# Unused matmuls in every gap of TensorE's plan, and a plan that reckons with half clock behind gaps

## The chip, the core and the metric

One core of one Trainium2 chip runs the whole program. The metric is the device time of one execution in microseconds. 0.2% of it, about 2.2 us, is what a measurement of this kernel can tell from no change.

## What is computed

An attention layer with a complex decaying state, cut to its recurrence, and behind it two feed-forward layers (FFN) over 3072 tokens, all in float32 (B = 4, H = 8, S = 768, D = 48):

```python
for t in range(S):
    ar, ai = a_re_n[:, :, t, :, None], a_im_n[:, :, t, :, None]   # normalised to at most 0.999
    new_re = ar * S_re - ai * S_im
    new_im = ar * S_im + ai * S_re
    S_re, S_im = new_re + k[:, :, t, :, None] * v[:, :, t, None, :], new_im
    y[:, :, t] = einsum('bhd,bhde->bhe', q[:, :, t], S_re)
x = y.transpose(0, 2, 1, 3).reshape(3072, 384)
h = x @ w_in;  x = (h * sigmoid(h)) @ w_out                        # 384 -> 2048 -> 384
h = x @ w_in2
g = where(h >= 1, h, where(h <= -1, 0, (h + 1) ** 2 / 4));  out = g @ w_out2
```

## The kernel before

The attention is cut into 12 units of 256 tokens (three in a row for each batch, all 8 heads at once). A unit normalises the decays, scans them into running products P (VectorE, mostly many small products in a chain), and forms Q times P and K divided by P. TensorE transposes these (`ptr`, from Q and from A), multiplies scores (`psc`), VectorE masks them (`AT`), TensorE multiplies the values (`py`) and the state of the unit (`pS`). Two small transposes serve the scan: `pt` (waits for RR) and `pe` (waits for X and brings back E).

The first FFN runs in 6 jobs of two units, 512 tokens each. Each float32 operand is split into a high and a low part of type fp32r, and every product takes three matmuls. A job has 16 steps f: 9 matmuls into `ph` (hidden layer), a gate on ScalarE that gives gH, a subtraction on VectorE that gives gL, and 9 matmuls that add into three sums `acc0` to `acc2`, which stay open from f = 0 to f = 15. The weights come as float64 bit patterns and are turned into float32 by VectorE, ScalarE and, for five of them, TensorE (`pw`). The second FFN (`pacc`) is alike and starts when the first has ended.

The order of instructions is set at build time by the class `Plan`. Each piece of work is a generator that asks for an engine, a duration and an earliest time. `go` always takes the request whose planned start plus its lag is smallest, and the instruction is written into its engine's queue at that moment. On the chip each queue runs in that order. So the planner's durations decide the order, and only that: on the chip an instruction starts when its engine and its data are there.

Unused matmuls exist already: the generator `awake` writes matmuls of 128x512 on the tile `junk` until the first FFN starts, each planned 3 us ahead of what it would wait for. The planner doubles TensorE's durations only until 16 of these have been planned (`cold`). The rows of the profile call these instructions `junk`.

Of the kernel before, what the change touches and what calls it, by code (L numbers as in the profile page):

```python
# [7 lines left out]
F32 = mybir.dt.float32  # L8
F32R = mybir.dt.float32r
I32 = mybir.dt.int32  # L10
# [10 lines left out]
PE, DVE, ACT, SP = "PE", "DVE", "ACT", "SP"  # L21


class Plan:
# [6 lines left out]
    def __init__(self):  # L31
        self.free = dict.fromkeys((PE, DVE, ACT, SP, "DMA"), 0.0)
        self.at = {}
        self.runs = []
        self.table = "exp"
        self.cold = lambda: False
        self.log = []
        self.rings = {"t": [2], "pa": [PAB], "ph": [PHB], "gH": [3], "gL": [3], "xq": [1], "sc": [4]}

# [30 lines left out]
    def dma(self, t, kb):  # L70
        b = self.free["DMA"] = max(self.free["DMA"], t + 1.4) + kb / 260.0
        return b + 0.8

    def go(self):
        while self.runs:
            best, moved = None, False
            for r in list(self.runs):
                while r in self.runs and (got := self.ready(r[2])) is not None:
                    self.step(r, got)
                    moved = True  # L80
                if r not in self.runs or isinstance(r[2], str) or len(r[2]) == 2:
                    continue
                e, us, t, *more = r[2]
                b = max(self.free[e], t)
                key = b + (more[1] if len(more) > 1 else r[0]())
                if best is None or key < best[0]:
                    best = key, b, r
            if best is None:
                if moved or not self.runs:
                    continue  # L90
                raise RuntimeError(str([(r[1].__name__, r[2]) for r in self.runs]))
            _, b, r = best
            e, us, t, *more = r[2]
            if e == PE and self.cold():
                us *= 2
            if more and more[0] and more[0] != self.table:
                self.table = more[0]
                us += 1.3
            self.log.append((b, e, us, r[1].__name__))
            self.free[e] = b + us  # L100
            self.step(r, b + us + 0.12)


def MM(n):
    return 0.69 if n == 512 else 0.37
# [704 lines left out]
class Ffn:  # L810
    def __init__(self, nc, tc, pools, w, plan):
        self.nc, self.tc, self.w, self.plan = nc, tc, w, plan
        self.W = [[None, None] for _ in range(8)]
        self.f = -1
        self.at = 0
        self.cp, self.wp, self.pp, self.dp, self.hp = pools
        self.cst = self.cp.tile([128, 3], F32, name="cst")
        for i, x in enumerate((-1.0, 0.5, 1.0)):
            nc.gpsimd.memset(self.cst[:, i:i + 1], x)
        self.fl_big = self.cp.tile([128, 32], F32, name="fl_big")  # L820

    def fetch(self, k, t0=0.0):
# [100 lines left out]
    def one(self, n, u, x, dst, tx, behind):  # L923
        nc, wp, pp, plan = self.nc, self.wp, self.pp, self.plan
        G, acc = {}, []
        p, N = u[0] // 2, 256 * len(u)
        part = N / 512
        o = u[0] % 2 * 256
        x = x[:, :, :, o:o + N]
        xH, xL = x[:, 0], x[:, 1]  # L930

        def outs(f):
            t0 = yield f"g{n}.{f}"
            if n == 0:
                t0 = max(t0, (yield f"w{f // 2 * 2 + 1}"))
            if f == 0:
                if n:
                    t0 = max(t0, (yield f"xo{n - 1}"))
                acc.extend(pp.tile([128, 512], F32, name=f"acc{j}", tag=f"acc{j}")[:, 0:N] for j in range(3))
            gH, gL, hH, hL = G.pop(f)  # L940
            oH, oL = self.wslices(f, 1)
            for j in range(3):
                w = slice(j * 128, (j + 1) * 128)
                t1 = yield PE, MM(N), t0
                nc.tensor.matmul(acc[j], oH[:, w], gH, start=f == 0, stop=False)  # L945
                nc.tensor.matmul(acc[j], oH[:, w], gL, start=False, stop=False)  # L946
                nc.tensor.matmul(acc[j], oL[:, w], gH, start=False, stop=f == 15)  # L947
                if f == 15:
                    T.append(t1)
            plan.drop("gH", hH, t1)  # L950
            plan.drop("gL", hL, t1)
            if u[-1] == UNITS - 1 and f % 2:
                plan.mark(f"used{f // 2 * 2 + 1}", t1)
            if f == 15:
                plan.add(XO, copies())

        T = []

        def copies():
            x2 = self.hp.tile([128, 3, 512], F32, name="x2", tag=f"x{p % 2}")[:, :, o:o + N]  # L960
            for j in range(3):
                t1 = yield ACT, 0.14 + 0.42 * part, T[j] + 0.2
                nc.scalar.copy(x2[:, j], acc[j])
                t2 = yield SP, 0.5, t1
                nc.sync.dma_start(dst[j * 128:(j + 1) * 128], x2[:, j])
            plan.mark(f"xo{n}", t1)
            t2 = plan.dma(t2, 262 * part)
            if u[-1] % 2:
                plan.mark(f"ffn{p}", t2)
                plan.mark(f"free x{p}", t2)  # L970

        def gate(f, ph, h, t1):
            hH, tH = yield "gH", 1
            gH = self.hp.tile([128, 512], F32R, name="gH", bufs=3)[:, 0:N]
            hL, tL = yield "gL", 1
            gL = self.hp.tile([128, 512], F32R, name="gL", bufs=3)[:, 0:N]
            t1 = yield ACT, 0.2 + 0.42 * part, t1 + 0.2, "silu"
            nc.scalar.activation(ph, ph, AF.Silu)  # L978
            t1 = yield ACT, 0.14 + 0.42 * part, max(t1, tH)
            nc.scalar.copy(gH, ph)  # L980
            t1 = yield DVE, 0.08 + 0.53 * part, max(t1, tL)
            nc.vector.tensor_tensor(gL, ph, gH, ALU.subtract)  # L982
            plan.drop("ph", h, t1)
            G[f] = gH, gL, hH, hL
            plan.mark(f"g{n}.{f}", t1)

        for f in range(16):
            tw = 0.0
            if n == 0:
                self.f = f  # L990
                tw = yield f"w{f // 2 * 2}"
            self.at = 1 + (u[0] + f / 16 * len(u)) / 2
            h, tf = yield "ph", 1
            ph = pp.tile([128, 512], F32, name="ph", tag="ph", bufs=PHB)[:, 0:N]
            t1 = yield from self.hidden(ph, f, xH, xL, max(tx, tw, tf), N)
            if u[-1] == UNITS - 1 and f % 2:
                plan.mark(f"used{f // 2 * 2}", t1)
            if f == 15 and u[-1] % 2:
                plan.mark(f"y{p}", t1)
            plan.add(GLAG, gate(f, ph, h, t1))  # L1000
            behind.append(outs(f))
            if len(behind) > DEEP:
                yield from behind.pop(0)
# [135 lines left out]
UR = 5  # L1139
SEP = 12  # L1140
SL = 0.75
AW = 0.25
WL = 1.4
WE = 0.45
FL = 0.2
# [12 lines left out]
def all_units(tc, plan, at, ff, xd2, out, fp, bad):  # L1158

    nc, wp = tc.nc, at.wp  # L1160
# [29 lines left out]
    def loada(i):  # L1190
        t = yield f"kT{i - 2}"
        t = max(t, (yield f"free{i - 2}"))
        yield from at.loada(i, t)
# [35 lines left out]
        yield "two1"  # L1229
        yield from flag_bad(nc, fp, at.pp, at, ff, plan, bad)  # L1230

    def awake():

        t = yield "P0"
        junk = at.pp.tile([128, 512], F32, name="junk", tag="acc0")
        while ff.f < 0:
            t = yield PE, AW, t - 3.0
            nc.tensor.matmul(junk, at.nid, at.nid.unsqueeze(1).to_broadcast([128, 4, 128]), start=True, stop=True)
            plan.at["warm"] = plan.at.get("warm", 0) + 1

    def second(k):
        t = max((yield f"used{k}"), (yield f"h{UNITS - 1}"))
# [6 lines left out]
        for k in range(n, 16, 2):  # L1249
            yield from second(k)  # L1250

    plan.cold = lambda: ff.f < 0 and plan.at.get("warm", 0) < 16
    with tc.manual_schedule(engines=None):
        plan.add(0.0, loads())
        for i in range(1, UNITS):
            if i > 1:
                plan.add(0.0, loada(i))
            plan.add(0.0, loadq(i, 0))
            plan.add(0.0, loadq(i, 1))
            plan.add(0.0, loadv(i))  # L1260
        for i in range(UNITS):
            plan.add(at.lag(i), at.unit(i, x))
            plan.add(0.0, at.knat(i))
        for n in range(3):
            me = [0]
            plan.add(urgent(me), weights(me))
        plan.add(behind, ffn())
        for n in range(2):
            plan.add(SL, seconds(n))
        for m in range(PAIRS):  # L1270
            plan.add(0.5, ff.prep(m, xd2[:, m * 512:(m + 1) * 512], ys))
        plan.add(FL, second_ffn())
        plan.add(0.5, flag())
        plan.add(1.2, awake())
        plan.go()


# [73 lines left out]
```

## Time and profile before

| | before |
|---|---|
| median of 3 runs | 1095.72 us (1095.23 to 1096.23) |
| the profiled execution's own time | 1097.16 us |
| its span, first to last instruction | 1095.5 us |
| mean granted TensorE clock | 0.978 |
| TensorE busy | 1018.3 us (93%) |
| VectorE busy | 797.7 us (73%) |
| ScalarE busy | 682.7 us (62%) |

Times in the views count from the span's start. Neighbouring matmuls overlap in the rows, so the time of one is read from a run of them. A row's bracket gives the engine's idle time before it, and what ended it.

### The profile page before, as it was taken

What the parts mean: (1) busy time and instruction counts of PE and PEld (TensorE: products, weight loads), DVE (VectorE), ACT (ScalarE), POOL (GpSimd) and SP (SyncE); (2) the same over time, 40 slices, a digit from 0 to 9 for tenths busy, and PEclk for the clock granted to TensorE, in tenths of its full rate; (3) what the DMA queues carried; (4) which work ended last, traced back from release to release, by engine and by line L of the source; (5) the groups of instructions that cost most, each with busy time, mean ns of one, the idle gap of its engine ahead of it and who ended that gap; (6) DMA issues with size and microseconds to landing.
All of it is one profiled execution on the core that took longest, in us unless ns stands there. A gap on an engine that the chain in (4) does not pass through costs nothing.

```text
span 1095.5 us, 14607 instructions
## 1 busy us (share of the span) xinstructions
PE 1018.3 (93%) x5486; PEld 840.2 (77%) x5486; DVE 797.7 (73%) x1492; ACT 682.7 (62%) x1048; POOL 1.4 (0%) x16
## 2 busy tenths in 40 slices
PE   0598698989999999999999999999999999999997
PEld 0476486778888888888888888887887878888896
DVE  6989999978888788898984179876556565555553
ACT  4456787768778686777846366665455454454443
POOL 0000000000000000000000000000000000000000
PEclk9789999899999999999999999999999999999999
DMA  5412350133131331313122165402002020000100
GB/s 215 156 40 87 137 202 22 43 124 116 37 102 65 124 98 69 116 37 102 65 80 74 40 218 182 173 1 59 1 1 58 1 58 1 14 15 1 29 1 32
DMA packets 55150, 82.03 MB, mean 75 GB/s; under 512 B 34592, under 2 KB 40480, under 8 KB 55072
## 3 DMA queue, kind: packets, MB, share of 16 engines
q1 hardware_dynamic: 54640, 80.53, 22.3%
q8 instruction: 45, 0.74, 0.3%
q10 hardware_dynamic: 432, 0.49, 0.1%
q14 instruction: 33, 0.27, 0.1%
HBM read 61.34 MB, written 17.30 MB: 72 GB/s over the span
## 4 chain that ended last, share of the span: by engine, by line
PE 72%; DVE 9%; ACT 8%; issue 1%; DMA 0%; SPq 0%; ACTq 0%; DVEq 0%
PE pacc L1086 16%; PE ph L903 10%; PE ph L905 10%; PE ph L904 10%; PE acc L945 5%; PE acc L946 5%; PE acc L947 5%; PE py L466 4%; PE psc L444 3%; PE ptr L372 2%; PE pS L537 2%; ACT L224 1%; ACT r L224 1%; DVE tt L176 1%; ACT ph L978 1%
## 5 line engine op out<-in xcount | busy, mean ns | idle before, releaser
L903 PE MATMUL ph<-x,wi 128*128 128x512 f32 x576 | 230.4, 400 | 3.2 <-DMA x<-xq 3.2
L904 PE MATMUL ph<-x,wi 128*128 128x512 f32 x576 | 225.7, 392 | 0.0
L905 PE MATMUL ph<-x,wi 128*128 128x512 f32 x576 | 225.6, 392 | 0.0
L1086 PE MATMUL pacc<-gH,wo 128*128 128x512 f32 x480 | 159.4, 390 | 0.0
L903 PEld LDWEIGHTS ph<-x,wi 128*128 128x128 f32 x576 | 109.0, 189 | 27.4 <-issue 2.4
L905 PEld LDWEIGHTS ph<-x,wi 128*128 128x128 f32 x576 | 108.7, 189 | 23.2
L904 PEld LDWEIGHTS ph<-x,wi 128*128 128x128 f32 x576 | 109.0, 189 | 20.7
L946 PE MATMUL acc<-gL,wo 128*128 128x512 f32 x288 | 113.9, 396 | 7.8 <-DVE gL L982 7.8
L945 PE MATMUL acc<-gH,wo 128*128 128x512 f32 x288 | 117.9, 409 | 0.0
L947 PE MATMUL acc<-gH,wo 128*128 128x512 f32 x288 | 114.0, 396 | 0.0
L1107 ACT ACTIVATE c<-c,cst 128x512 f32<-128x512 f32 x96 | 69.5, 724 | 63.8 <-DVE c L1104 63.8
L1109 DVE TENSOR_TENSOR g<-c,l 128x512 f32<-128x512 f32 x96 | 66.5, 693 | 56.4 <-ACT c L1107 56.3
L1113 DVE TENSOR_TENSOR gL<-g,gH 128x512 fp32r<-128x512 f32 x96 | 66.5, 692 | 55.0 <-ACT gH L1111 53.9
L1104 DVE TENSOR_SCALAR c<-ph 128x512 f32<-128x512 f32 x96 | 66.3, 690 | 52.8 <-ACT l L1102 52.6
L1086 PEld LDWEIGHTS pacc<-gH,wo 128*128 128x128 f32 x480 | 90.1, 188 | 18.6
L1102 ACT ACTIVATE l<-ph,cst 128x512 f32<-128x512 f32 x96 | 65.8, 685 | 60.1 <-PE ph L905 59.9
L978 ACT ACTIVATE ph<-ph 128x512 f32<-128x512 f32 x96 | 57.5, 599 | 72.2 <-PE ph L905 71.7
L1111 ACT CAST gH<-g 128x512 fp32r<-128x512 f32 x96 | 59.6, 621 | 64.3 <-DVE g L1109 64.3
L982 DVE TENSOR_TENSOR gL<-ph,gH 128x512 fp32r<-128x512 f32 x96 | 65.5, 686 | 45.6 <-ACT gH L980 45.2
L1086 PE MATMUL pacc<-gL,wo 128*128 128x512 f32 x240 | 94.6, 394 | 1.7 <-DVE gL L1113 0.8
L946 PEld LDWEIGHTS acc<-gL,wo 128*128 128x128 f32 x288 | 55.0, 191 | 18.2 <-DVE gL L982 8.3
L947 PEld LDWEIGHTS acc<-gH,wo 128*128 128x128 f32 x288 | 54.9, 191 | 11.9
(176 smaller groups left out, 1715.7 us busy)
## 6 DMA issues: line engine op xcount, KB each, us to landing
raw<-in_w_dram SPq DMA_DIRECT2D x32, 768.0 KB, 5.9
A<-in_a_dram SPq DMA_DIRECT2D x12, 768.0 KB, 4.7
kd<-A SPq DMA_DIRECT2D x10, 768.0 KB, 4.0
KN<-kd SPq DMA_DIRECT2D x20, 384.0 KB, 3.8
qt<-in_qk_dram SPq DMA_DIRECT2D x12, 384.0 KB, 3.1
kt<-in_qk_dram SPq DMA_DIRECT2D x12, 384.0 KB, 4.6
vt<-in_vn_dram SPq DMA_DIRECT2D x24, 192.0 KB, 2.5
xd<-x SPq DMA_DIRECT2D x18, 256.0 KB, 2.2
```

Source lines behind the costliest of these rows:

```text
L903: nc.tensor.matmul(ph, iH[:, j], xH[:, j], start=j == 0, stop=False, skip_group_check=True)
L904: nc.tensor.matmul(ph, iH[:, j], xL[:, j], start=False, stop=False, skip_group_check=True)
L905: nc.tensor.matmul(ph, iL[:, j], xH[:, j], start=False, stop=j == 2, skip_group_check=True)
L945: nc.tensor.matmul(acc[j], oH[:, w], gH, start=f == 0, stop=False)
L946: nc.tensor.matmul(acc[j], oH[:, w], gL, start=False, stop=False)
L947: nc.tensor.matmul(acc[j], oL[:, w], gH, start=False, stop=f == 15)
L978: nc.scalar.activation(ph, ph, AF.Silu)
L1086: nc.tensor.matmul(o, l, r, start=f == 0 and k == 0, stop=f == 15 and k == 2)
L1104: nc.vector.tensor_scalar(c, ph, 1.0, -1.0, ALU.min, ALU.max)
L1107: nc.scalar.activation(c, c, AF.Square, bias=self.cst[:, 1:2], scale=0.5)
L1109: nc.vector.tensor_tensor(g, c, l, ALU.add)
L1113: nc.vector.tensor_tensor(gL, g, gH, ALU.subtract)
```

## The change

Four things are changed.

- `awake` and `cold` go. In their place `Plan.idle` looks, at every TensorE request, at the planned gap ahead of it (8 us of it at most). From 0.6 us on it writes unused matmuls for the gap, one per 0.235 us, half as many for the first 4 us if the planned clock is low.
- `Plan.clocked` keeps a list of planned busy time and doubles a TensorE duration while the planned clock counts as low. This holds for the whole plan, not only for the start.
- An unused matmul multiplies by a tile of zeros. Until the first sum of a job has begun, `fill` writes nothing (or, before the first FFN, to the tile `junk`); from then to f = 15 it adds its zeros into the open sum acc0.
- Ahead of these, one memset of the zero tile.

```diff
-        self.cold = lambda: False
+        self.slow, self.past, self.fill = True, [], None
...
+    def idle(self, b):
+        g = min(b - self.free[PE], 8.0) - 0.1
+        if g < AK or b < 25.0:
+            return
+        n = int(g / AW if not self.slow else min(g, 4.0) / AW / 2 + max(0.0, g - 4.0) / AW)
+        if n and self.fill(n):
+            self.past.append((b - g, b))
+
+    def clocked(self, b, us):
+        p = self.past
+        while p and p[0][1] < b - 4.0:
+            p.pop(0)
+        n = sum(y - max(x, b - 4.0) for x, y in p)
+        self.slow = n < (3.7 if self.slow else 2.2)
+        us *= 1 + self.slow
+        p.append((b, b + us))
+        return us
...
-            if e == PE and self.cold():
-                us *= 2
-            if more and more[0] and more[0] != self.table:
+            if e == PE:
+                self.idle(b)
+                us = self.clocked(b, us)
+            elif more and more[0] and more[0] != self.table:
...
+            if f % 15 == 0:
+                self.open = None
...
+            if f == 0:
+                self.open = [acc[0], n]
...
-AW = 0.25
+AW = 0.235
+AK = 0.6
...
-    def awake():
-        t = yield "P0"
-        junk = at.pp.tile([128, 512], F32, name="junk", tag="acc0")
-        while ff.f < 0:
-            t = yield PE, AW, t - 3.0
-            nc.tensor.matmul(junk, at.nid, at.nid.unsqueeze(1).to_broadcast([128, 4, 128]), start=True, stop=True)
-            plan.at["warm"] = plan.at.get("warm", 0) + 1
+    def fill(n):
+        if ff.open is None:
+            return False
+        if not ff.open:
+            ff.open.append(at.pp.tile([128, 512], F32, name="junk", tag="acc0"))
+        for _ in range(n):
+            nc.tensor.matmul(ff.open[0], at.nid, ff.zero.unsqueeze(1).to_broadcast([128, 16, 32]), start=len(ff.open) == 1,
+                             stop=len(ff.open) == 1, skip_group_check=True)
+        return True
...
-    plan.cold = lambda: ff.f < 0 and plan.at.get("warm", 0) < 16
...
-        plan.add(1.2, awake())
```

TensorE's queue had 78 unused matmuls and has 212: 186 ahead of the first FFN, 26 within its first job, none later. Here is TensorE's order in unit 0, from the first `pe` to the scores. `ptr` are the transposes, from Q and then from A. Before:

```order
L308 MATMUL pe<-ident,X 128x48 x2
L1238 MATMUL junk<-nid 128x512 x9
L372 MATMUL ptr<-ident,Q 96x128 x8
L1238 MATMUL junk<-nid 128x512 x4
L372 MATMUL ptr<-ident,Q 96x128 x8
L1238 MATMUL junk<-nid 128x512
L372 MATMUL ptr<-ident,A 96x128 x8
L1238 MATMUL junk<-nid 128x512
L372 MATMUL ptr<-ident,A 96x128 x8
L1238 MATMUL junk<-nid 128x512
L444 MATMUL psc<-QT,KT 128x128 x4
```

The same place now:

```order
L1267 MATMUL junk<-zero,nid 128x512 x18
L329 MATMUL pe<-ident,X 128x48 x2
L1267 MATMUL junk<-zero,nid 128x512 x33
L393 MATMUL ptr<-ident,Q 96x128 x8
L1267 MATMUL junk<-zero,nid 128x512 x14
L393 MATMUL ptr<-ident,Q 96x128 x8
L1267 MATMUL junk<-zero,nid 128x512 x11
L393 MATMUL ptr<-ident,A 96x128 x8
L1267 MATMUL junk<-zero,nid 128x512 x7
L393 MATMUL ptr<-ident,A 96x128 x8
L1267 MATMUL junk<-zero,nid 128x512 x7
L465 MATMUL psc<-QT,KT 128x128 x4
```

Nothing but unused matmuls has been put in: between the first transposes and the scores 39 for 7. Unit 1 has the same numbers ahead of its scores.

The second place is in the first job, around the `pe` of unit 3, where the last two weights are converted (`pw`). TensorE before:

```order
L871 MATMUL pw<-raw,ids 128x384 x2
L880 MATMUL pw<-wo_1502,nid 128x384 x2
L903 MATMUL ph<-x,wi_1242 128x512
L904 MATMUL ph<-x,wi_1242 128x512
L905 MATMUL ph<-x,wi_1242 128x512
L308 MATMUL pe<-ident,X 128x48 x2
L871 MATMUL pw<-raw,ids 128x384 x2
L880 MATMUL pw<-wi_1556,nid 128x384 x2
L945 MATMUL acc_1011<-gH,wo_1119 128x512
```

And now:

```order
L895 MATMUL pw<-raw,ids 128x384 x2
L904 MATMUL pw<-wo_1629,nid 128x384 x2
L1267 MATMUL acc_1121<-zero,nid 128x512 x3
L895 MATMUL pw<-raw,ids 128x384 x2
L329 MATMUL pe<-ident,X 128x48 x2
L904 MATMUL pw<-wi_1661,nid 128x384 x2
L927 MATMUL ph<-x,wi_1350 128x512
```

The three `ph` matmuls ahead of `pe` have gone behind it, three unused ones stand in their place, and the last conversion has moved ahead of `pe`.

The order of the rest of the attention shifts too, since the planned times do. This table counts, from TensorE's queue, how many `ph` and `acc` matmuls of the first FFN stand ahead of some instructions of the attention:

| ahead of | before | now |
|---|---|---|
| pe of unit 3 | 189 | 180 |
| first transposes of Q, unit 3 | 216 | 225 |
| first transposes of Q, unit 4 | 324 | 306 |
| pt of unit 5 | 396 | 363 |
| first transposes of Q, unit 10 | 1209 | 1113 |
| first transposes of Q, unit 11 | 1293 | 1368 |

## Rows read from the trace of the kernel before

**Rows 1.** The page, part 1: busy us of each engine, share, instructions.

```profile
PE 1018.3 (93%) x5486; PEld 840.2 (77%) x5486; DVE 797.7 (73%) x1492; ACT 682.7 (62%) x1048; POOL 1.4 (0%) x16
```

**Rows 2.** Windows: length, busy us of engines, granted clock, DMA share, GB/s.

```profile
30.00:34.00 4.00, 3.90 (x11) 2.75 (x11) 3.69 (x10) 1.06 (x2) 0.00 (x0) 1.00 0.00 0
40.00:60.00 20.00, 15.47 (x67) 12.18 (x69) 18.50 (x34) 11.80 (x15) 0.00 (x0) 0.59 0.62 236
134.00:140.00 6.00, 5.29 (x15) 4.20 (x16) 5.79 (x8) 5.92 (x7) 0.00 (x0) 0.59 0.00 0
196.00:204.00 8.00, 7.43 (x19) 5.25 (x18) 7.76 (x17) 3.46 (x8) 0.00 (x0) 0.57 0.00 0
200.00:280.00 80.00, 77.23 (x490) 64.57 (x490) 67.37 (x137) 59.97 (x87) 0.00 (x0) 0.95 0.31 97
240.00:246.00 6.00, 5.42 (x16) 3.95 (x17) 5.86 (x14) 5.28 (x7) 0.00 (x0) 0.72 0.44 131
280.00:500.00 220.00, 217.26 (x1339) 180.33 (x1335) 186.72 (x399) 170.75 (x246) 0.00 (x0) 1.00 0.26 82
640.00:660.00 20.00, 20.00 (x90) 16.57 (x89) 18.98 (x27) 13.55 (x26) 0.00 (x0) 1.00 0.51 189
```

**Rows 3.** Waits of TensorE from 100 to 260 us: total, times, longest.

```profile
PE acc L946 <- DVE gL L982: 7.8, 1, 7.8
```

**Rows 4.** Timeline of TensorE, 30 to 54 us: start, us, operation, count.

```profile
30.24 3.66 PE L1238 MATMUL junk<-nid 128*128 128x512 f32 x9
41.06 1.91 PE L372 MATMUL ptr<-ident,Q 128*96 128x128 f32 x8 [7.16 <-DVE Q L354]
...
53.44 0.80 PE L444 MATMUL psc<-QT,KT 96*128 96x128 f32 x2 [0.70 <-ACT KT L376]
```

**Rows 5.** Timeline of TensorE, 76 to 92 us, unit 1.

```profile
76.93 8.10 PE L1238 MATMUL junk<-nid 128*128 128x512 f32 x35
87.07 1.35 PE L372 MATMUL ptr<-ident,Q 128*96 128x128 f32 x8 [2.04 <-DVE Q L354]
88.07 3.97 PE L1238 MATMUL junk<-nid 128*128 128x512 f32 x10
91.88 0.60 PE L372 MATMUL ptr<-ident,Q 128*96 128x128 f32 x4
```

**Rows 6.** Waits of VectorE from 54 to 70 us.

```profile
DVE AT L450 <- PE psc L444: 2.0, 2, 1.2
DVE xq L479 <- ACT x L477: 1.0, 1, 1.0
DVE tt L172 <- ACT X L277: 0.7, 1, 0.7
```

**Rows 7.** Timeline of TensorE, 195 to 203 us.

```profile
195.33 0.35 PE L308 MATMUL pe<-ident,X 48*128 48x48 f32 x2 [1.82 <-DVE X L179]
...
198.78 0.63 PE L945 MATMUL acc<-gH,wo 128*128 128x512 f32 x1
...
202.62 0.63 PE L903 MATMUL ph<-x,wi 128*128 128x512 f32 x1
```

**Rows 8.** Timelines: Q of unit 3, RR of unit 5, and TensorE behind them.

```profile
204.14 1.75 DVE L354 TENSOR_TENSOR Q<-A,qt 128x1536 f32<-128x1536 f32 x1
...
207.31 0.93 PE L372 MATMUL ptr<-ident,Q 128*96 128x128 f32 x7
...
277.23 0.25 DVE L268 TENSOR_TENSOR RR<-tt 128x96 f32<-128x96 f32 x1
...
277.88 0.39 PE L273 MATMUL pt<-ident,RR 128*96 128x128 f32 x2
```

**Rows 9.** Waits of VectorE from 200 to 280 us.

```profile
DVE M L384 <- ACT r L224: 4.2, 2, 3.1
DVE R L547 <- PE pS L537: 2.3, 2, 1.7
```

More of the change, by code (lines that the diff above doesn't have):

```diff
@@ L819, in __init__ @@
             nc.gpsimd.memset(self.cst[:, i:i + 1], x)
+        self.zero = self.cp.tile([128, 32], F32R, name="zero")
+        nc.vector.memset(self.zero.bitcast(I32), 0)
+        self.open = []
         self.fl_big = self.cp.tile([128, 32], F32, name="fl_big")
@@ L1230, in flag @@
         yield from flag_bad(nc, fp, at.pp, at, ff, plan, bad)
-    def awake():
-        t = yield "P0"
-        junk = at.pp.tile([128, 512], F32, name="junk", tag="acc0")
-        while ff.f < 0:
-            t = yield PE, AW, t - 3.0
-            nc.tensor.matmul(junk, at.nid, at.nid.unsqueeze(1).to_broadcast([128, 4, 128]), start=True, stop=True)
-            plan.at["warm"] = plan.at.get("warm", 0) + 1
+    def fill(n):
[7 more added lines that the diff above has]
+        return True
+    plan.fill = fill
     def second(k):
```

## The prediction

> **What bounds the kernel now.** I read the page's busy shares first, then the windows, then who waits for whom, then the timelines around the places that the change touches. The shares alone mislead: TensorE is busy 93% of the span and VectorE 73% [rows 1], yet the two take turns as the limit. In the windows VectorE is nearly full while attention unit 0 and 1 run (18.50 of 20 us at 40 to 60 us) and TensorE is not (15.47, at a granted clock of 0.59). From 280 us on TensorE is the limit: 217.26 of 220 us busy, VectorE 186.72 [rows 2]. The reader should see that the granted clock reads 1.00 in all the late windows. What half clock costs lies before 250 us, and half of it in a stretch where TensorE is the engine that waits. There its longest wait is 7.8 us for the first gL of the first FFN [rows 3], and the clock behind it, from 134 to 140 us, is 0.59 [rows 2].
>
> **Where the clock fell.** Four stretches count: 40 to 60 us, 134 to 140, 196 to 204 (0.57) and 240 to 246 (0.72) [rows 2]. Each lies behind idle time or sparse work. A row of dense work also shows the two levels. 9 unused matmuls at 30 us took 3.66 us, 407 ns each; 35 at 77 us took 8.10 us, 231 ns each [rows 4, 5]. That is 1.2 against 2.4 GHz. The granted clock of 30 to 34 us reads 1.00 all the same [rows 2]; the durations decide, so the first 30 us ran at the lower level. The Trainium skill (TensorE: Matmul & The Clock Gate, "Seeing it yourself", the note on trace caveats) warns that clock events in a trace have been unreliable; this trace agrees at 30 us. By the clock column the 51 unused matmuls that now stand ahead of the first transposes would take 12 us, by the durations up to 21.
>
> **The price of an unused matmul.** In a dense stretch, 640 to 660 us, 90 matmuls of 128x512 take 20.00 us, 0.222 us each [rows 2]. The change has 212 of them where there were 78: 186 ahead of the first FFN, 26 within its first job. One within the sum costs 0.222 us if TensorE would have worked, and nothing if it would have waited.
>
> **Step 1, units 0 and 1 (186 against 78 unused matmuls).** VectorE limits here, so a busier TensorE costs only what it makes VectorE wait, and a faster one gives only what VectorE waited for TensorE: 2.0 us for the scores, 1.0 for ACT's copy of the values, 0.7 for the copy of a transpose, together 3.7 us at 54 to 70 us [rows 6]. That is the most to be won. Against it: from the first transposes at 41.06 to the scores at 53.44 us [rows 4] there stand 39 unused matmuls now, 7 before. The 32 extra take 7.4 us at 231 ns. At full clock the real work of 40 to 60 us would need 15.47 x 0.59 = 9.1 us, which leaves 10.9 us of room in 20, some 6.7 in those 12.4 us. So the scores come about 0.7 us later if the clock is up, and more if it isn't: behind the 33 unused matmuls there is idle time again before the transposes, and 2.04 us of such idle time at 85 us was followed by a fall within the next matmuls (10 of them took 3.97 us) [rows 5]. 14 at 407 ns instead of 231 are 2.5 us more. Once the scores start, they run at full clock instead of half. I take -1.7 us, near the middle; bounds -3.7 (every wait gone) and +2 (scores late, nothing regained).
>
> **Step 2, from the first gL to the pe of unit 3.** Between these two VectorE has the same 109 instructions in both orders, and in before pe waits for it 1.8 us (195.33 us) [rows 7]. So that point comes at the same distance after the first gL; time that TensorE saves ahead of it turns into a longer wait. This holds for the 0.59 stretch at 134 to 140 us too, and the 7.8 us wait isn't filled: there the list of open sums is empty until the first sum has begun. What changes is how much is done by then: 189 FFN matmuls before, 180 now, plus 20 unused ones. 9 x 0.222 = **+2.0 us** are owed; the other 11 lie in waits. Bounds: 0, if the 9 would not have limited, and 4.4, if all 20 are paid.
>
> **Step 3, from there to the query transposes of unit 3.** Six unused matmuls more: **+1.3 us** (0 if they fall in a wait). Won back is the half clock of 196 to 204 us: 7.43 us busy at 0.57 are 3.2 us lost [rows 2]; 9 matmuls took 3.84 us from 198.78 to 202.62 [rows 7], against 2.0 at full clock. But the transposes at 207.31 us need Q, which ends at 205.89 [rows 8], so 1.4 us of it can be used and the rest becomes a wait. I take **-1.2 us**, bounds -1.4 and 0 (the clock falls as before).
>
> **Step 4, units 4 and 5.** The new order brings attention forward: 363 FFN matmuls ahead of the pt of unit 5, 396 before. The other 33 - 9 = 24, 5.3 us, come after it, so VectorE has 5.3 us less to reach the same point. In before it got there 0.40 us ahead of TensorE (277.48 against 277.88) [rows 8]. But it idled 80 - 67.37 = 12.6 us from 200 to 280 us [rows 2]. Of its waits there 2.3 us are for TensorE's pS and shrink with a shorter queue; 4.2 us are for ScalarE's r and don't [rows 9]. Bounds 0 and +5; **+0.4 us**, since 5.3 of 12.6 us can be found.
>
> **Step 5, units 5 to 10.** At unit 10 the lead is 1209 - 1113 = 96 matmuls. 63 more than at unit 5 are 14 us out of 33.3 us of idle VectorE from 280 to 500 us [rows 2]. Bounds 0 and +5, **+0.4 us**. With unit 11 the lead is gone (75 matmuls more ahead of it than before), where 27 sum matmuls, 6 us, stand between its last values and the next job's x.
>
> **Sum.** -1.7 + 2.0 + 1.3 - 1.2 + 0.4 + 0.4 = +1.2 us. It is made against the profiled execution (span 1095.5, time 1097.16 us); the median is 1.44 us below that time, and the same +1.2 on it gives **1096.9 us**. A measurement of this kernel tells about 0.2% (2.2 us) from no change, so this is no change.
>
> **Rivals.**
> - *VectorE becomes the limit in units 4 and 5.* TensorE then waits at the pt of unit 5 for the 5 us of step 4. For it: the slack of 0.40 us, and 4.2 us of VectorE's waits that hang on ScalarE. Against it: 12.6 us of idle time. It decides if VectorE wins back less than some 3 us of these. 1096.9 + 4.6 = 1101.5 us, slower.
> - *The unused matmuls meet no wait.* All 26 are paid, 5.8 us instead of the 3.3 in steps 2 and 3: 1099.4 us. For it: 10 unused ones ahead of 91.88 us [rows 5] ran without a gap up to the work behind them. Against it: TensorE waits of its own ahead of that place, the 1.8 us of pe [rows 7] among them. The Trainium skill (the same page, "Step-by-step: what each phase is for") states that matmuls stay in program order, only weight loads being pulled ahead; by that rule an unused matmul in front of work that is ready delays it, which is this rival.
> - *They don't hold the clock up* in 196 to 204 us: the -1.2 is missing, 1098.1 us.
> - *The new order fits better than I count.* VectorE's 3.7 us of step 1 go entirely (-2.0), steps 4 and 5 cost nothing (-0.8), and 240 to 246 us stays at full clock (5.42 x 0.28 = -1.5): 1092.6 us, faster. For it: a plan that knows of half clock places TensorE's work nearer to where it runs. Against it: no unused matmul stands at 240 us.
>
> **Chances.** My forecast 0.45 (0.35 of it within 0.2%, 0.08 slower, 0.02 faster); VectorE limits 0.18; all 26 paid 0.09 (0.07 slower); clock not held 0.06 (0.04 slower); better fit 0.22 (0.21 faster). That is faster 0.23, same 0.40, slower 0.37. The likeliest case alone spans 1095 to 1099 us. For 8 in 10 the range takes in the better fit with 1.5 us below it and the VectorE case: 1091 to 1102 us.
>
> **What the profile of the changed kernel would show.** Step 1: the first gL at 131 to 134 us instead of 134, and VectorE's waits for the scores at 54 to 70 us about halved. Step 2: still some 7 us of wait for the first gL and half clock behind it; pe of unit 3 at the same distance from the first gL. Step 3: granted clock 1.00 around 196 to 204 us, and a short wait of the query transposes for Q. Steps 4 and 5: waits of pt and ptr for VectorE below 1 us each. It is wrong if pt of unit 5 waits over 3 us, if TensorE idles over 7 us from 280 to 600 us, or if the clock falls in new places behind the unused matmuls.

## The result and the profile after

The changed kernel takes **1107.49 us** in the median of 4 runs (1106.59 to 1108.95), beside 1095.54 us for the kernel before in the same comparison (4 runs). The ratio is 1.0106, 95% interval 1.0091 to 1.0121: slower by 11.9 us, outside the predicted range. The profiled execution has a span of 1107.2 us and a mean granted clock of 0.991 (before 0.978).

The page, part 1, beside [rows 1]:

```profile
PE 1040.0 (94%) x5620; PEld 856.8 (77%) x5620; DVE 797.9 (72%) x1493; ACT 686.3 (62%) x1050; POOL 1.4 (0%) x16
```

A kernel whose clock is higher and whose TensorE share is larger has become slower. The windows, with the columns of [rows 2], say where:

```profile
40.00:60.00 20.00, 18.87 (x119) 14.97 (x120) 18.69 (x35) 12.76 (x18) 0.00 (x0) 1.00 0.63 237
196.00:204.00 8.00, 8.00 (x36) 6.55 (x35) 8.00 (x10) 5.67 (x9) 0.00 (x0) 1.00 0.00 0
200.00:280.00 80.00, 73.62 (x480) 60.29 (x478) 67.56 (x150) 63.34 (x90) 0.00 (x0) 0.96 0.31 97
240.00:246.00 6.00, 5.24 (x26) 4.06 (x25) 4.47 (x5) 5.60 (x7) 0.00 (x0) 0.93 0.33 97
252.00:255.00 3.00, 3.00 (x13) 2.36 (x12) 3.00 (x4) 2.93 (x5) 0.00 (x0) 0.58 0.17 67
280.00:500.00 220.00, 209.97 (x1293) 173.99 (x1293) 184.36 (x385) 167.24 (x241) 0.00 (x0) 0.99 0.28 86
354.00:358.00 4.00, 4.00 (x21) 3.14 (x20) 3.83 (x11) 3.16 (x5) 0.00 (x0) 0.63 1.01 339
```

The granted clock is up where unused matmuls were put (40 to 60 and 196 to 204 us). But TensorE idles 6.4 us from 200 to 280 us, where it was 2.8, and 10.0 us from 280 to 500, where it was 2.7 [rows 2]. These 10.9 us of new idle time are almost as much as the whole loss. Behind two of the waits the clock falls in new places, at 252 and at 354 us. The four largest of TensorE's waits from 240 to 480 us (total, times, longest):

```profile
PE ptr L393 <- ACT QT L397: 5.5, 5, 1.7
PE psc L465 <- ACT KT L397: 2.4, 2, 2.0
PE acc L971 <- ACT gH L1008: 2.2, 1, 2.2
PE pe L329 <- ACT X L324: 1.1, 1, 1.1
```

All four hang on ScalarE, which is busy 62% of the span. Three of the waits for QT follow one another around 350 us. TensorE's timeline there (L393 are the attention's transposes, L971 at 355.19 us is the next job's first sum):

```profile
345.67 0.39 PE L973 MATMUL acc<-gH,wo 128*128 128x512 f32 x1
...
347.71 0.39 PE L929 MATMUL ph<-x,wi 128*128 128x512 f32 x1
349.84 0.64 PE L393 MATMUL ptr<-ident,Q 128*96 128x128 f32 x4 [1.74 <-ACT QT L397]
351.74 0.64 PE L393 MATMUL ptr<-ident,Q 128*96 128x128 f32 x4 [1.26 <-ACT QT L397]
353.57 1.97 PE L393 MATMUL ptr<-ident,A 128*96 128x128 f32 x8 [1.20 <-ACT QT L397]
355.19 0.78 PE L971 MATMUL acc<-gH,wo 128*128 128x512 f32 x1
```

And ScalarE's at the same place (L245 are the roots of unit 6, a logarithm and an exponential, each with a table load; L991 are the copies that free the job's three sums):

```profile
343.74 0.94 ACT L245 ACTIVATE r<-M,bl 128x768 f32<-128x768 f32 x1
344.69 1.28 ACT L245 ACT_TABLE_LOAD   x1
345.99 0.94 ACT L245 ACTIVATE r<-r,bl 128x768 f32<-128x768 f32 x1
346.95 1.28 ACT L1006 ACT_TABLE_LOAD   x1
348.24 0.58 ACT L1006 ACTIVATE ph<-ph 128x512 f32<-128x512 f32 x1
348.74 1.05 ACT L397 COPY QT<-ptr 96x512 f32<-96x512 f32 x1
...
351.98 0.61 ACT L991 COPY x<-acc 128x512 f32<-128x512 f32 x1
```

An FFN job has ended here. Its last sum matmul (345.67 us) has run by 346.1 us; the next job's sums need the three copies, and the transposes need the copies of QT, which free their buffers. All of these stand on ScalarE behind the roots with their table loads. TensorE has three groups of transposes in a row and no FFN work between them.

### The profile page after: what moved, and what is told of

Read it like the earlier page. It is cut to its first block, busy times and chain, and to the rows that moved or that the text cites. A ratio compares the mean times of both kernels' runs of the same rounds, so it can differ in the third digit from the quotient of the medians.

```text
span 1107.2 us, 14874 instructions
## 1 busy us (share of the span) xinstructions
PE 1040.0 (94%) x5620; PEld 856.8 (77%) x5620; DVE 797.9 (72%) x1493; ACT 686.3 (62%) x1050; POOL 1.4 (0%) x16
## 4 chain that ended last, share of the span: by engine, by line
PE 61%; ACT 7%; DVE 5%; issue 1%; ACTq 0%; DVEq 0%
PE pacc L1114 16%; PE ph L927 9%; PE ph L929 9%; PE ph L928 9%; PE acc L971 4%; PE acc L973 4%; PE acc L972 4%; PE py L487 2%; PE psc L465 2%; PE pS L558 1%; PE ptr L393 1%; ACT L245 1%; ACT r L245 1%; DVE c L1132 1%; DVE g L1137 1%
## 5 line engine op out<-in xcount | busy, mean ns | idle before, releaser
L971 PE MATMUL acc<-gH,wo 128*128 128x512 f32 x288 | 117.9, 409 | 2.2 <-ACT gH L1008 2.2
L971 PEld LDWEIGHTS acc<-gH,wo 128*128 128x128 f32 x288 | 54.7, 190 | 14.0 <-ACT gH L1008 2.6
```

## Experiments

All comparisons are with the kernel before, run on the same chip.

### Order or unused matmuls?

**e1.** The doubled duration is left out for a part of the plan:

```diff
-        us *= 1 + self.slow
+        us *= 1 + (self.slow and not 120.0 < b < 245.0)
```

> The changed kernel with one term taken out: between 120 and 245 us of its plan the planner no longer counts a doubled duration for TensorE. It still puts unused matmuls into the gaps: 151 ahead of the first FFN as in the order listing, 25 within it (the changed kernel has 26). From the first FFN on the order of all engines is then the order of before. Theory A (the loss of 11.9 us comes from the order that the new price leads the planner into): back at 1093 to 1098 us, that is 1095.5 - 2.9 for the stretch ahead of the first FFN, plus nothing to 25 x 0.222 = 5.6 for the unused matmuls; I take 1094. Rival B (the unused matmuls inside the FFN cost the loss, by their own time or by holding up what stands behind them): 25 of 26 are still there, so 1104 us or more.

(Ahead of the first FFN there are 186 unused matmuls, not the 151 written there.) Measured: 1093.59 us, ratio 0.9986 (0.9976 to 0.9995). 25 of the unused matmuls in the FFN are there, and the loss is gone. Theory A holds, rival B falls.

**e2, e3.** The unused matmuls in the FFN are counted by the planner but not written, in the order of the change (e2) and in that of e1 (e3, which has both edits):

```diff
+        if len(ff.open) == 2:
+            return True
         for _ in range(n):
             nc.tensor.matmul(ff.open[0], at.nid,
...
```

> The changed kernel, with the 26 unused matmuls within the FFN counted by the planner but not written; the order of all other instructions is exactly that of the changed kernel. Theory A (order): 1102 to 1107.5 us, at most 26 x 0.222 = 5.8 us less than the changed kernel's 1107.5, and less than that where they stood in gaps that are empty now. Rival B (unused matmuls): most of the loss goes, 1098 us or less.

> Both edits: no doubled duration between 120 and 245 us of the plan, and the unused matmuls within the FFN not written, so that only those ahead of the first FFN stay and the rest is the order of before. By both theories the stretch ahead of the first FFN is worth about 2.9 us: 1092.6 us, 1091 to 1094.5. Beside the run without the price alone it shows what 25 unused matmuls cost in the old order: A expects 0 to 5.6 us, B 10 us or more.

Measured: e2 1107.92 us, ratio 1.0115 (1.0098 to 1.0132); e3 1093.21 us, 0.9977 (0.9967 to 0.9987). In neither order can the effect of the unused matmuls in the FFN be told from zero (-0.4 and +0.4 us). Most of what they win is lost again at once, as the windows of e1 and of e3 from 193 to 201 us show:

```profile
193.00:201.00 8.00, 7.37 (x30) 5.38 (x31) 7.76 (x17) 2.96 (x7) 0.00 (x0) 1.00 0.00 0
```

```profile
193.00:201.00 8.00, 7.43 (x18) 5.31 (x19) 7.76 (x17) 3.38 (x8) 0.00 (x0) 0.58 0.00 0
```

With them (e1, first row) the clock is up, 30 matmuls run where 18 did, and then the transposes of unit 3 wait 1.3 us for Q.

**e4.** Each of the 26 is written twice:

```diff
-        for _ in range(n):
+        for _ in range(n * len(ff.open)):
```

> The changed kernel's order, with every unused matmul within the FFN written twice (52 in place of 26). Theory A: 1107.5 us plus nothing to 26 x 0.222 = 5.8, so 1107.5 to 1113; where the first 26 lay in gaps that are longer than they, the next 26 are partly free too. Rival B: the loss grows by about as much again, 1117 us or more.

Measured: 1114.37 us, ratio 1.0171 (1.0154 to 1.0188), 6.9 us over the changed kernel, a little above A's upper end. The first 26 cost nothing that can be told (e2); the next 26 were paid in full (0.26 us each). Of the 6.9 us, 6.1 are there at the first transposes of unit 3 (211.44 us against 205.37), which is 0.23 us for each; where the rest comes from isn't traced.

### Is it the price of half clock?

**e5.** The kernel before, with one number changed:

```diff
-    return 0.69 if n == 512 else 0.37
+    return 0.70 if n == 512 else 0.37
```

> The kernel before with one number of its planner changed: a step of three FFN matmuls is counted at 0.70 us in place of 0.69. None of the change is in it: no unused matmul in the FFN, no price for half clock. Theory C (the order of before is a narrow fit of its numbers, and any change of the costs loses it): 1103 us or more, with waits of TensorE between 240 and 480 us, about 10 us of them. Rival D (the price of half clock is what bends the order): within 3 us of 1095.5.

Measured: 1120.47 us, ratio 1.0226 (1.0201 to 1.0251). A hundredth of a microsecond in the plan costs 25 us on the chip, more than the whole change. Theory C's 1103 or more holds, rival D falls. The largest waits are of the same kind (TensorE, 240 to 480 us):

```profile
PE ptr L372 <- ACT QT L376: 11.8, 6, 5.5
```

**e8.** All rules of the change, with the planner's numbers set anew (the FB of the run is left out here, since it moved nothing):

```diff
-XO = 0.3
+XO = 0.2
-QO = 0.1
+QO = 0.15
-UO = [0.0, 0.0, 0.0, 0.0, 0.0, 0.0, 0.0, 0.0, 0.0, 0.0, 0.0, -0.1]
-FO = [0.0, 0.1, 0.0, 0.0, 0.0, 0.0]
+UO = [0, 0, 0, 0, 0, 0, 0.1, 0, 0, 0, 0, 0.0]
+FO = [0, 0.1, 0.2, 0, 0, 0]
```

> The changed kernel with all of its rules (the price of half clock and unused matmuls in every gap, 26 of them in the FFN) and five of the planner's numbers set anew: XO 0.3 to 0.2, QO 0.1 to 0.15, FO of the third pair 0 to 0.2, UO of unit 6 0 to 0.1 and of unit 11 -0.1 to 0 (FB 0.6 to 0.55 changes nothing). Before unit 5's pt stand 396 FFN matmuls again (363 in the changed kernel). Theory C (any rule does as well once the numbers fit it): 1092 to 1099, TensorE's waits between 240 and 480 us back to 2 to 5 us. Rival D (the price of half clock bends the order whatever the numbers): 1103 or more.

Measured: 1096.12 us, ratio 1.0001 (0.999 to 1.0012). So with the price of half clock an order as good as before's can be had (rival D falls twice). Theory C fits both runs: the numbers of before fit one set of costs narrowly, and one cost moved by 0.01 us is enough to lose the order. That any change of the costs would do it was not tested. The gain of e1 and e3 isn't in e8: it is level with the kernel before.

### Single places in ScalarE's queue?

**e6.** The changed kernel's order, one piece of it moved. ScalarE's queue, before the move and after it:

```diff
 ACTIVATE ph<-ph 128x512
-ACT_TABLE_LOAD
-ACTIVATE r<-M,bl1 128x768
-ACT_TABLE_LOAD
-ACTIVATE r<-r,bl1 128x768
 CAST gH<-ph 128x512
-ACT_TABLE_LOAD
-ACTIVATE ph<-ph 128x512
 ACTIVATE ph<-ph 128x512
 CAST gH<-ph 128x512
+ACTIVATE ph<-ph 128x512
 CAST gH<-ph 128x512
+ACT_TABLE_LOAD
+ACTIVATE r<-M,bl1 128x768
+ACT_TABLE_LOAD
+ACTIVATE r<-r,bl1 128x768
 COPY QT<-ptr 96x4x128
```

> The changed kernel's order, written out, with its unused matmuls at the same places, and one piece moved on ScalarE and VectorE alone: the silu, the gH and the gL of three FFN steps stand ahead of unit 4's roots (two table loads and two 0.94 us activations), which held up gH at 244 to 248 us. Theory A1 (single places in ScalarE's queue make the loss): TensorE's waits of 2.2 and 0.6 us at 249 and the half clock behind them, some 8 matmuls at 0.43 in place of 0.23 us, go: 1107.5 - 4.4 = 1103. Rival A2 (with the FFN short of steps the wait only moves on to the next attention matmul): within 1.5 us of 1107.5.

Measured: 1109.74 us, ratio 1.0123 (1.0098 to 1.0148). A1 falls: slower than the changed kernel, not 4.4 us faster. The wait for gH at 249 us is gone, and now the copies of QT stand behind the roots. TensorE's timeline:

```profile
249.28 0.39 PE L980 MATMUL ph<-x,wi 128*128 128x512 f32 x1
253.66 2.00 PE L444 MATMUL ptr<-ident,Q 128*96 128x128 f32 x8 [4.00 <-ACT QT L448]
255.32 0.78 PE L978 MATMUL ph<-x,wi 128*128 128x512 f32 x1
```

The two rows around the transposes belong to one FFN step, whose x and weights were there. The second stood behind the transposes for 4.0 us and did not pass them. The Trainium skill (TensorE: Matmul & The Clock Gate, "Step-by-step: what each phase is for") says that matmuls stay in program order and only weight loads are pulled ahead; this row agrees.

**e7.** Besides, at the ends of the second and third job the three copies of the sums are put in one piece (ScalarE), and the next job's first nine sum matmuls ahead of the transposes (TensorE, here at 348 us):

```diff
-MATMUL ptr<-ident,Q 96x128 x4
-MATMUL ptr<-ident,Q 96x128 x4
...
 MATMUL acc0<-gH,wo0 128x512
 MATMUL acc0<-gL,wo0 128x512
 MATMUL acc0<-gH,wo0 128x512
...
+MATMUL ptr<-ident,Q 96x128 x4
+MATMUL ptr<-ident,Q 96x128 x4
```

> The same piece moved, and two more: at the ends of the FFN's second and third pair (348 and 452 us) the three copies of the sums stand in one piece ahead of the attention's copies on ScalarE, and the next pair's first nine sum matmuls stand ahead of the transposes (348) or of the transposes of K (452) on TensorE. Theory A1: beside the 4.4 us above, of the waits of 1.7, 1.3 and 1.2 us at 350 to 354 about 2 are covered by these nine matmuls (9 x 0.227 = 2.0), the half clock of 354 to 357 goes (about 1.5), and of the 2.0 us at 456 most: 1107.5 - 4.4 - 5 = 1098. Rival A2: within 2 us of 1107.5.

Measured: 1114.42 us, ratio 1.0166 (1.014 to 1.0193). Worse again, and outside A2's 2 us as well; A1 falls a second time. TensorE's waits for QT and KT from 240 to 480 us are 11.5 us in e6 and 11.3 in e7, where the changed kernel has 7.9: what is moved ahead on ScalarE makes something else stand behind the roots. That this is all that e7 loses is not shown.

### How the job ends lie to the roots

What remained was the place of the job ends in the attention's course. A theory A2 (attention ahead of the FFN costs, the further the more) stood against A3 (a job's end among an even unit's roots, transposes of Q and transposes of K costs).

**e9, e10.** All rules of the change, other numbers. Two of those of e9:

```diff
-LG = 0.2
-KO = 0.8
+LG = 0.1
+KO = 0.85
```

Besides these, UO of unit 1 and FO of the third pair are 0.1 in e9. e10 has AO 0.2, KO 0.7, and FO of the third and fifth pair -0.2 and -0.1.

> The changed kernel with all its rules and four of the planner's numbers set otherwise (LG 0.2 to 0.1, KO 0.8 to 0.85, UO of unit 1 0 to 0.1, FO of the third pair 0 to 0.1), chosen because the attention stands still further ahead: ahead of pt of units 5 and 10 stand 327 and 1014 FFN matmuls (changed kernel 363 and 1032, before 396 and 1116). Of the next pair's FFN matmuls 0, -30, -51 and -78 stand ahead of the first transposes of Q of units 4, 6, 8 and 10 (changed kernel 18, 6, -24, -39; before 36, 33, 24, 57), and 36, 21, -6, -30 ahead of the last transposes of K (changed kernel 57, 30, 27, 12; before 87, 84, 78, 87): the ends of the later pairs fall behind these transposes, no longer among them. Theory A2 (attention ahead of the FFN is what costs, the further the more): 1110 us or more. Theory A3 (what costs is that the end of an FFN pair falls into the stretch from the roots of an even unit to its transposes of K, where ScalarE has both to serve): 1096 to 1103, and TensorE's waits between 340 and 480 us under 4 us (changed kernel 10).

> The changed kernel with all its rules and four numbers set otherwise (AO 0.1 to 0.2, KO 0.8 to 0.7, FO of the third pair 0 to -0.2 and of the fifth 0 to -0.1), chosen because the FFN stands further ahead than in the kernel before: 399 and 1143 FFN matmuls ahead of pt of units 5 and 10, and 39, 108, 72 and 108 of the next pair's ahead of the first transposes of Q of units 4, 6, 8 and 10. Theory A2: 1097 us or less, since the attention is later than in any of the others. Theory A3: pair ends lie ahead of the roots, so no waits there; 1093 to 1099 as well, if they meet no other busy stretch of ScalarE. Together with the run on attention far ahead: A2 wants the two on either side of 1107.5, A3 wants both below it.

Measured: e9 1105.58 us, ratio 1.0096 (1.0079 to 1.0113); e10 1101.10 us, 1.0053 (1.0035 to 1.007). A2 falls on both sides: the attention stands further ahead in e9 and it is no slower than the changed kernel; it stands further back in e10 than in the kernel before, and e10 is slower than that. A3's times are missed as well (1096 to 1103 and 1093 to 1099). Its waits came true in e9 (from 340 to 480 us none is over 1 us), but this order has a wait of its own at 245 us. TensorE, 240 to 480 us:

```profile
PE ptr L393 <- DVE x L502: 6.9, 1, 6.9
```

The wait ends with VectorE's x at 244.79 us, but VectorE stood itself behind ScalarE's roots, those of unit 4. Its timeline:

```profile
243.72 0.96 DVE L405 TENSOR_TENSOR M<-M,r 128x768 f32<-128x768 f32 x1 [3.53 <-ACT r L245]
...
244.79 0.55 DVE L502 TENSOR_TENSOR x<-py,x 112x384 fp32r<-112x384 f32 x1
```

And a job's end lies there: of the next job's matmuls 0 stand ahead of the first transposes of Q of unit 4 and 36 ahead of the last ones of K. That is A3's own stretch, which its forecast of the time left out.

**e11, e12.** Two cleaner pairs. e11 has the order of e1 written out up to about 290 us and is planned freely from there with two other numbers; e12 is to the changed kernel what e11 is to e1.

```diff
+            forced = self.turn < len(ORDER)
+            if forced:
+                r = next(r for r in self.runs if r[3] == ORDER[self.turn])
...
-AO = 0.1
+AO = 0.2
-FO = [0.0, 0.1, 0.0, 0.0, 0.0, 0.0]
+FO = [0, 0.1, 0, 0, 0.1, 0]
```

(e12: LG 0.1, and FO of the fifth pair -0.2.)

> As the run with the price left out (its order is that of before from the first FFN on), with that order written out up to about unit 5's scores and planned freely from there, with two numbers set otherwise (AO 0.1 to 0.2, FO of the fifth pair 0 to 0.1). From there on the attention moves ahead as in the changed kernel: of the next pair's FFN matmuls 27, -15 and -36 stand ahead of the first transposes of Q of units 6, 8 and 10, and 39, 27 and 12 ahead of the last transposes of K (changed kernel 6, -24, -39 and 30, 27, 12; before 33, 24, 57 and 84, 78, 87). Unused matmuls in the FFN: 27. Theory A3 (pair ends among an even unit's roots and transposes make TensorE wait): 1093.6 plus two to three ends at 2 to 4 us, 1098 to 1104, with 5 us or more of new waits between 330 and 570 us. Rival A4 (the loss is made up to unit 4, by the wait at 249 us and what follows from it): within 1.5 us of 1093.6.

> The changed kernel with its order written out up to about 290 us and planned freely from there, with two numbers set otherwise (LG 0.2 to 0.1, FO of the fifth pair 0 to -0.2): the ends of the later pairs then fall behind the transposes, with -3, -69 and -63 FFN matmuls of the next pair ahead of the first transposes of Q of units 6, 8 and 10 and 27, -3 and -6 ahead of the last ones of K. Unused matmuls in the FFN: 28. Theory A3: the wait at 249 us stays (2.2 and 0.6 us), those at 456 us go and of those at 350 to 354 most: 1100 to 1104. Rival A4: 1106 or more.

Measured: e11 1107.65 us, ratio 1.0111 (1.0092 to 1.013); e12 1102.60 us, 1.0059 (1.004 to 1.0078). Both go the way that A3 expects (e11 beyond its upper end), neither as A4. e12 keeps the changed kernel's idle time at unit 4 (table below) and 6.4 us of loss against before. e11 loses 14 us against e1 although its order is the same up to 290 us, unused matmuls included. (With the same order the two profiled executions stand 2.3 us apart at the first transposes of unit 4, 246.8 and 249.1 us; single executions can differ by so much.) Its timelines at the end of the second job, ScalarE and TensorE (line numbers differ in this kernel: L275 roots, L1021 copies of the sums, L427 copies of QT, L423 transposes):

```profile
342.92 0.56 ACT L1021 COPY x<-acc 128x512 f32<-128x512 f32 x1
...
345.90 0.94 ACT L275 ACTIVATE r<-M,bl 128x768 f32<-128x768 f32 x1
...
348.99 1.92 ACT L427 COPY QT<-ptr 96x512 f32<-96x512 f32 x2
350.71 1.11 ACT L1021 COPY x<-acc 128x512 f32<-128x512 f32 x2
```

```profile
350.07 1.98 PE L423 MATMUL ptr<-ident,Q 128*96 128x128 f32 x8 [4.57 <-ACT QT L427]
```

The copies of QT, for which TensorE waits 4.57 us, and two of the three copies of the sums stand behind the roots. In e1 the copies of the sums end well ahead of them:

```profile
332.93 1.95 ACT L991 COPY x<-acc 128x512 f32<-128x512 f32 x3 [1.88 <-PE acc L973]
...
342.92 0.94 ACT L245 ACTIVATE r<-M,bl 128x768 f32<-128x768 f32 x1
```

The windows from 330 to 570 us of the changed kernel, of e1, of e11 and of e12, in this order:

```profile
330.00:570.00 240.00, 231.17 (x1446) 191.92 (x1447) 201.36 (x432) 178.50 (x264) 0.00 (x0) 0.99 0.27 85
```

```profile
330.00:570.00 240.00, 237.83 (x1495) 197.96 (x1494) 204.75 (x440) 177.94 (x263) 0.00 (x0) 1.00 0.28 86
```

```profile
330.00:570.00 240.00, 227.92 (x1438) 188.43 (x1437) 204.98 (x439) 179.21 (x262) 0.00 (x0) 0.99 0.28 86
```

```profile
330.00:570.00 240.00, 235.39 (x1463) 196.41 (x1462) 205.00 (x436) 183.03 (x266) 0.00 (x0) 0.99 0.28 86
```

A table of the orders. "Ahead of Q" counts, from TensorE's queue, the FFN matmuls of the next job that stand ahead of the first transposes of Q of units 4, 6, 8 and 10 (negative: the job itself still has so many to go); "ahead of K" those ahead of the last transposes of K. Idle is TensorE's, the window's length less its busy time.

| kernel | median us | ahead of Q | ahead of K | idle 225 to 265 us | idle 330 to 570 us |
|---|---|---|---|---|---|
| before | 1095.5 | 36, 33, 24, 57 | 87, 84, 78, 87 | 2.8 | 2.2 |
| e1 | 1093.6 | 36, 33, 24, 57 | 87, 84, 78, 87 | 2.5 | 2.2 |
| e8 | 1096.1 | 27, 27, 75, 36 | 84, 87, 120, 87 | 3.7 | 3.3 |
| changed | 1107.5 | 18, 6, -24, -39 | 57, 30, 27, 12 | 6.4 | 8.8 |
| e2 | 1107.9 | 18, 6, -24, -39 | 57, 30, 27, 12 | 6.6 | 7.2 |
| e5 | 1120.5 | 36, 27, 12, -18 | 84, 45, 27, 27 | 3.0 | 16.9 |
| e11 | 1107.7 | 36, 27, -15, -36 | 87, 39, 27, 12 | 2.4 | 12.1 |
| e12 | 1102.6 | 18, -3, -69, -63 | 57, 27, -3, -6 | 6.8 | 4.6 |
| e9 | 1105.6 | 0, -30, -51, -78 | 36, 21, 0, -30 | 12.8 | 3.3 |
| e10 | 1101.1 | 39, 108, 72, 108 | 90, 138, 123, 135 | 2.8 | 6.8 |

(At unit 8 of e9 the queue has 0 ahead of K, not the -6 written there.) At units 6, 8 and 10: where all three job ends have less than 50 matmuls and more than none ahead of K, TensorE idles 7.2 to 16.9 us from 330 to 570 us; where at least two lie outside, 2.2 to 6.8. The bounds of this stretch were chosen after the runs. At unit 4 the same can be read: with 27 or more ahead of Q it idles 2.4 to 3.7 us from 225 to 265 us, with 18 it idles 6.4 to 6.8, with none 12.8. It is no sharp rule: the end at unit 6 in e9 (-30 and 21) lies in the stretch and no wait over 1 us follows, and e10's idle time has another source (3.1 us of pe waiting for VectorE at 537 us).

## Why the prediction was wrong, point by point

- **Step 1** (units 0 and 1, -1.7 us): the mechanism was right, the size small. It measured -2.8: the wait for the first gL ends at 131.87 us instead of 134.71, inside the forecast 131 to 134. VectorE's waits at 54 to 70 us fell from 3.7 us [rows 6] to 0.9, as much as was won; the one for the scores fell from 2.0 to 0.2. (The middle of the bounds given there is -0.85, not -1.7.) The waits in the changed kernel:

```profile
DVE xq L500 <- ACT x L498: 0.7, 1, 0.7
DVE AT L471 <- PE psc L465: 0.2, 1, 0.2
```

- **Step 2** (first gL to pe of unit 3): right in mechanism and size. The 7.8 us wait of [rows 3] is still there, and pe of unit 3 comes at the same distance behind it, 60.5 us (60.6 before). It is 3.0 us earlier than before with 9 FFN matmuls fewer done (2.0 us), so the lead of 2.8 us has shrunk to 1.0: +1.8 us, forecast +2.0. TensorE's first gL before, then the changed kernel with this point and those of steps 3 and 4:

```profile
134.71 0.79 PE L946 MATMUL acc<-gL,wo 128*128 128x512 f32 x1 [7.85 <-DVE gL L982]
```

```profile
131.87 0.79 PE L972 MATMUL acc<-gL,wo 128*128 128x512 f32 x1 [7.83 <-DVE gL L1010]
...
192.36 0.32 PE L329 MATMUL pe<-ident,X 48*128 48x48 f32 x2
...
205.37 0.82 PE L393 MATMUL ptr<-ident,Q 128*96 128x128 f32 x6
...
269.19 0.38 PE L294 MATMUL pt<-ident,RR 128*96 128x128 f32 x2
```

- **Step 3** (+1.3 - 1.2 = +0.1): the clock from 196 to 204 us is 1.00, as forecast, but the size was wrong, to the other side. The transposes of unit 3 come 1.9 us earlier than in [rows 8] with 9 FFN matmuls more done (225 against 216, 2.0 us), a lead of 3.9 us: -2.9 us. The forecast let most of the time won end in a wait for Q. Between pe and these transposes 45 FFN matmuls stand now where 27 stood, they take up that time, and no wait is left. In the order of before the wait comes, 1.3 us (e1).
- **Step 4** (units 4 and 5, +0.4, bounds 0 and +5) failed in the same way as step 5. pt of unit 5 comes 8.7 us earlier than in [rows 8] and doesn't wait at all, so VectorE did find the time. What waited was TensorE for gH behind ScalarE's roots at 249 us: 3.6 us more idle time from 200 to 280, and half clock behind it (3.00 x 0.42 = 1.3 us at 252 us): +4.9 us. The half clock that before had from 240 to 246 us is not won back; it only comes earlier:

```profile
236.00:242.00 6.00, 5.16 (x15) 3.74 (x16) 5.96 (x11) 4.86 (x6) 0.00 (x0) 0.72 0.44 131
```

- **Step 5** (units 5 to 10, +0.4, bounds 0 and +5) is the step that failed. It asked whether VectorE could run ahead, and counted ScalarE nowhere: it put TensorE's waits for ScalarE's copies at nothing. It measured 7.3 us more idle time from 280 to 500 us and 4.00 x 0.37 = 1.5 us of half clock at 354 us: +8.8 us. From the lead of 3.9 us at unit 3, steps 4 and 5 lead to 9.8 us of loss; the spans of the two profiled executions differ by 11.7. The other 1.9 us are not traced; single executions of one order lie that far apart too (e11).
- **The rivals.** "All 26 paid" falls: without them the time is the same (e2). "They don't hold the clock up" falls: it is 1.00. "VectorE limits in units 4 and 5" put 5 us into that stretch, where 4.9 were lost, but pt didn't wait and the engine was ScalarE: that the size is near is luck. "Better fit" falls for the new order; in the old order the same unused matmuls are 2.0 (e1) and, without those in the FFN, 2.4 us (e3) faster than before.
- The text's own alarm was hit: TensorE idles 10.0 us within 280 to 500 us alone, where over 7 us from 280 to 600 would make it wrong, and the clock falls in new places, though behind these waits and not behind unused matmuls.
- **The clock at 30 us.** The 1.00 of 30 to 34 us [rows 2] is no sign of an unreliable clock in this trace. The column reads 1.00 also where TensorE has not begun:

```profile
0.00:10.00 10.00, 0.00 (x0) 0.00 (x0) 1.62 (x4) 4.93 (x8) 1.44 (x16) 1.00 0.79 310
```

The trace's clock records begin at 33.1 us, and they agree with the matmuls: from 30.83 to 32.97 us the nine start 0.43 us apart, the last two, at 33.28 and 33.51 us, 0.23 us. The 407 ns are a mean over both levels. That the stretch before ran at the lower level stays right.

**What is shown and what isn't.** Shown: the 26 unused matmuls in the FFN cost nothing that can be told (e2), the stretch ahead of it wins 2.4 us (e3; beside the unused matmuls a few instructions stand in another order there), and the order alone makes the loss (e1 against the changed kernel, 13.9 us; e2). Shown too: it isn't the price of half clock as such (e5, e8), and with one order up to 290 us the later part makes a difference of 14 us (e11). That job ends among an even unit's roots are the cause is supported by e11, e12, the table and e9's wait at unit 4, with the exception of e9's unit 6; it is not shown. Each of these orders differs in more than the job ends, and a kernel in which they alone are moved was not run. Nor was one with more buffers for the transposes.

The best kernel of the study is e3: the order of before from the first FFN on, with unused matmuls ahead of it only, 1093.21 us, 0.23% faster than before.

## What to carry to other kernels

Where a greedy planner writes the order, a change of its costs is above all a new draw of the order. Price that before the instruction that was added: run the change in the old order, and the new order without the change. Another cost, even one meant to be truer, can lose as long as the numbers tuned beside it are the old ones. And when attention or another chain is brought ahead, count every engine on it, also the one that is busy 62%. Here the copies that stood in ScalarE's queue behind a 4.4 us piece (two table loads of 1.28 us and two activations of 0.94) came after it, and held up TensorE with all that stood behind the waiting matmul.

## What the runs showed unexpectedly

- Idle time of TensorE isn't always followed by half clock. Before, 2.04 us of it at 85 us was followed by 10 unused matmuls in 3.97 us [rows 5]. In the changed kernel 1.74 and 1.56 us of it, behind a row of 33 unused matmuls, are followed by 14 in 3.60 and 3.59 us, 257 ns each, at a granted clock of 1.00. Step 1 had allowed 2.5 us for a fall at this place; none came, which fits its winning more than was forecast. The timeline of the changed kernel:

```profile
30.06 8.17 PE L1267 MATMUL junk<-zero,nid 128*128 128x512 f32 x33
39.97 1.05 PE L393 MATMUL ptr<-ident,Q 128*96 128x128 f32 x8 [1.74 <-DVE Q L375]
40.77 3.60 PE L1267 MATMUL junk<-zero,nid 128*128 128x512 f32 x14
```

- A cost of 0.70 instead of 0.69 us in a build-time plan moved the measured time by 2.3%.
